# First attention unit taken pair of heads by pair of heads, in a fused attention and two-MoE kernel

## The chip, the cores and the metric

The kernel runs on one core of a Trainium2 chip. The metric is device time in microseconds, the median of three runs. Five engines work side by side, each through its own list of instructions in order: TensorE (PE; its weight loads are PEld), VectorE (DVE), ScalarE (ACT), GpSimd (POOL) and SyncE (SP, which issues most transfers). They wait for each other by semaphores.

## The reference

```python
kv = np.einsum('bhsd,bhse->bhde', k, v)           # linear attention, 4 batches, 8 heads, 576 rows, width 64
out = np.einsum('bhsd,bhde->bhse', q, kv)
x = out / sqrt(mean(out * out) + 1e-6) * g_norm    # then 2304 rows of 512 (8 heads x 64)
# first MoE, dense: 4 experts, hidden 1024, p = domain_probs / sum
out += p[:, e:e + 1] * (np.maximum(x @ w1[e], 0.0) @ w2[e])
# second MoE: 8 experts, one chosen per row by cosine logits; its softmax weight times relu(x @ w1) @ w2
```

## The kernel before, in words

All matmuls of the two MoEs work on split numbers: a value is cast to a high part (ACT, line 61), and the rest is the low part (VectorE or POOL, line 62). Each product is then three matmuls: high by high, high by low, low by high.

The 2304 rows are six units of 384 rows, three tiles of 128 each. The first layer of a unit and half an expert is four blocks (hidden slices of 128) of 12 matmuls each, 128x384 (line 802, `plain_unit`); relu and split of the hidden values are lines 786 and 789. The second layer takes each tile in two halves of six matmuls, 128x512 (line 909, `l2_unit`); line 915 scales its result by the normalized probabilities into the accumulator the first time, line 918 adds to it later. From the second pair of units on, a Strassen scheme (line 814) replaces the plain blocks.

The program's order is written by hand: `run_steps` takes a list of TensorE steps, each with a nominal length, and puts the entries of `todo` behind the step at which their due time has passed. So the due times set the order in each engine's list, not the moment at which something runs. `att(tiles)` makes the attention of a tile a series of such entries: `qt_unit` (transpose q, line 142; copy by ACT, line 148; it also asks for a later q tile), `x_unit` (state product, line 159; square, line 173; sum, line 175; root, line 186), `x_norm` (lines 187 to 198 and 181) and `xt_unit` (transpose, line 204; ACT's scaled copy, line 208). `x_norm` is spread over the list behind its `x_unit`, and the next tile's `qt_unit` stands ahead of the previous tile's `xt_unit`.

Weights come by a stream of transfers through four buffers (`issue`, lines 551 to 567; w1 at line 560, w2 at line 564). A buffer is asked for again when its block has been split, so SP waits for VectorE, and what is behind it in SP's list waits too. `take` hands out the blocks in stream order.

The first unit has code of its own (lines 983 to 1038). The stream's first four blocks are k and v of batch 0, one pair of heads each: four rows of a head side by side in a partition, and the last 64 rows of all heads apart (`load_tail`, line 96). `kv_unit` multiplies k and v of a pair over the rows (lines 107 and 110) and copies the result into a block-diagonal state (line 113). Then the three tiles of q are transposed, multiplied by the state (line 159), squared, summed and normalized together, transposed and split into the first-layer input (lines 204, 211, 212). `heat` are matmuls whose result nobody reads. k and v of batch 1 go into `en_b`, a buffer that later holds the second MoE's embeddings; their four `kv_unit`s stand between the four blocks of the first unit's first layer (due at 1.5, 3.5, 5.5, 7.5), and the split of the second-layer weights (`fill_w2`) and the normalization of the probabilities `dp` (`norm_probs`, lines 1041 to 1044) stand there too. Tile 3's attention runs beside the second layer of the first phase; tiles 4 and 5 beside the next phase, which is the same unit with the other half of the expert.

Of the kernel before, what the change touches and what calls it, by code (L numbers as in the profile page):

```python
# [20 lines left out]
def attn_moe_moe_kernel(ctx: ExitStack, tc: tile.TileContext, q, k, v, g_norm, dprobs, w1, w2, emb, tau, w1b, w2b, out):  # L21
# [646 lines left out]
    stream += [("kv", 0, n) for n in range(NP)] + raws(0, 0) + raws(0, 1) + raws(0, 0)  # L668
# [280 lines left out]
    def run_steps(steps, todo, pace):  # L949
        todo = sorted(todo, key=lambda x: x[0])  # L950
        at = 0.0
# [32 lines left out]
    for _ in range(RAW):  # L984
        issue()
    Q0 = TS

    def q_first_raw(t):
        return xr.rearrange("p u c n -> p (u c n)")[:, D * t:D * t + D]

    for t in range(Q0):
        load_q(t, nc.sync, q_first_raw(t))
    for m in kv_bd:
        nc.gpsimd.memset(m, 0.0)
    for i in range(2):
        nc.gpsimd.dma_start(out=g2[64 * i:64 * i + 64], in_=g_norm.rearrange("(d o) -> d o", o=1))
    for p in range(NP):
        kv_unit(0, p)
        heat(2)
    def load_kv1(p):  # L1000
        load_kv(1, p, en_b[:, 2 * p:2 * p + 2].rearrange("p i n -> p (i n)"))

    load_tail(1)
    for p in range(NP):
        load_kv1(p)
    nc.sync.dma_start(out=dp, in_=dprobs.rearrange("(t p) e -> p t e", p=128))
    for t in range(Q0, Q0 + QB):
        load_q(t, nc.sync)
    qx = [acc[TS + t].rearrange("p (a n) -> p a n", a=NP) for t in range(Q0)]
    px = [psp.tile([128, H, DH], F32, name=f"psx{t}", tag=("x0", "x1", "l20")[t]) for t in range(Q0)]  # L1010
    ms = st_p.tile([128, TS, H], F32, name="ms3", tag="ms3", bufs=1)

    def q_first(t):
        ps = q_transpose(t, ("tp", "l10", "l11")[t])
        (nc.vector.tensor_copy if t % 2 == 0 else nc.scalar.copy)(qx[t], ps)

    def x_first(t):
        x_mm(t, qx[t], px[t])
        x_s[t] = acc[t].rearrange("p (h d) -> p h d", h=H)
        nc.scalar.activation(out=x_s[t], in_=px[t], func=ACTF.Square)  # L1020
        nc.vector.tensor_reduce(out=ms[:, t], in_=x_s[t], axis=AX.X, op=ALU.add)

    q_first(0)
    q_first(1)
    for t in range(Q0):
        if t + 2 < Q0:
            q_first(t + 2)
        x_first(t)
    heat(14, psp.tile([128, 128], F32, name="warm2", tag="kv"))
    ri = rms_end(*rms_start(ms, [128, TS, H], "s"))  # L1030
    w1_blocks(0, 0)
    for part in range(3):
# [278 lines left out]
```

## Time and profile before

| | |
|---|---|
| median of three runs | 1152.33 us (1151.47 to 1153.69) |
| the profiled execution | 1154.61 us, span 1152.7 us |
| busy in the span | PE 1110.8 us (96%), DVE 764.9 (66%), ACT 559.5 (49%), POOL 276.4 (24%) |
| mean granted TensorE clock | 0.989 of full speed |

The span is the time from the first to the last instruction; the profiled execution's time is 1.9 us longer. A timeline row gives start and length in us, the engine, the line, what is written from what, and how often; in brackets stands how long the engine was idle before and what ended that wait. A matmul's length holds its way through the array, so rates are read from start to start. A float32 matmul shows as two records, a transpose as one. Between 0 and 80 us TensorE is idle for the loads, for the first unit's normalization, and twice for 1.4 us for an attention tile; after that it hardly waits until the routing at 840 us.

### The profile page before, as it was taken

To read this page: it belongs to the slowest core of one execution; us is meant where nothing else is said; L and a number is where in the kernel's file an instruction comes from. 1 tells how busy PE (TensorE), PEld (TensorE's weight loads), DVE (VectorE), ACT (ScalarE), POOL (GpSimd) and SP (SyncE) were. 2 spreads that over 40 slices of the span, in tenths; PEclk is the share of its full clock that TensorE was granted. 3 is DMA by queue.
4 is the path that set the end of the run, shared out by engine and by line. 5 is a ranking of instruction groups with operands and counts; after the bars stand their busy time and mean duration, and the time that the engine had idled before them with its cause. 6 is when DMAs were issued, how large, how long until landed. Compare 5 with 4: busy or idle time off the path is not lost. (4 is left out here: it accounts for less than half of the span.)

```text
span 1152.7 us, 17304 instructions
## 1 busy us (share of the span) xinstructions
PE 1110.8 (96%) x5905; PEld 972.7 (84%) x5905; DVE 764.9 (66%) x1340; ACT 559.5 (49%) x1000; POOL 276.4 (24%) x325
## 2 busy tenths in 40 slices
PE   7999999999999999999999999999968999999996
PEld 7889898888888898889889998899857878888875
DVE  3467665566996788766796787765876548763662
ACT  3545446444455344444455444332336348763663
POOL 3002332222441322322243322200011112112111
PEclk9999999999999999999999999999989999999999
DMA  9523244221334232221232222123164159855871
GB/s 263 142 55 110 83 147 149 72 82 47 107 113 142 88 92 63 67 74 56 82 119 83 82 83 65 55 73 119 37 240 135 38 163 376 315 172 169 281 239 43
DMA packets 89730, 141.79 MB, mean 123 GB/s; under 512 B 17365, under 2 KB 52181, under 8 KB 89504
## 3 DMA queue, kind: packets, MB, share of 16 engines
q1 hardware_dynamic: 82032, 115.66, 31.1%
q0 software_dynamic: 7600, 24.93, 6.5%
q8 instruction: 49, 0.80, 0.3%
q14 instruction: 49, 0.40, 0.1%
HBM read 178.31 MB, written 10.49 MB: 164 GB/s over the span
## 5 line engine op out<-in xcount | busy, mean ns | idle before, releaser
L909 PE MATMUL bank<-w2h,hh 128*128 128x512 f32 x576 | 227.4, 395 | 1.4 <-ACT hh L786 1.4
L909 PE MATMUL bank<-w2h,hl 128*128 128x512 f32 x576 | 225.5, 391 | 0.0
L909 PE MATMUL bank<-w2l,hh 128*128 128x512 f32 x576 | 225.0, 391 | 0.0
L62 DVE TENSOR_TENSOR w2l<-raw,w2h 128x1024 fp32r<-128x1024 f32 x100 | 120.3, 1225 | 91.5 <-ACT w2h L61 90.9
L814 PE MATMUL bank<-xth,w1h 128*128 128x384 f32 x560 | 145.9, 341 | 5.5 <-ACT s L821 2.6
L814 PE MATMUL bank<-xth,w1l 128*128 128x384 f32 x560 | 142.6, 335 | 0.0
L814 PE MATMUL bank<-xtl,w1h 128*128 128x384 f32 x560 | 142.5, 335 | 0.0
L918 DVE SCALAR_TENSOR_TENSOR acc<-bank,dp,acc 128x512 f32<-128x512 f32 x123 | 91.9, 747 | 59.9 <-PE bank L909 59.6
L909 PEld LDWEIGHTS bank<-w2h,hl 128*128 128x128 f32 x576 | 108.1, 188 | 24.8 <-DVE hl L789 1.8
L909 PEld LDWEIGHTS bank<-w2h,hh 128*128 128x128 f32 x576 | 108.2, 188 | 24.5 <-ACT hh L786 3.7
L909 PEld LDWEIGHTS bank<-w2l,hh 128*128 128x128 f32 x576 | 108.2, 188 | 21.0
L814 PEld LDWEIGHTS bank<-xth,w1h 128*128 128x128 f32 x560 | 99.3, 188 | 11.0 <-ACT s L821 3.8
L62 DVE TENSOR_TENSOR w1l<-raw,w1h 128x512 fp32r<-128x512 f32 (+2 forms) x137 | 89.5, 669 | 22.5 <-ACT w1h L61 22.5
L61 ACT CAST w2h<-raw 128x1024 fp32r<-128x1024 f32 x100 | 102.9, 1056 | 1.8 <-DMA raw<-in_moe_w_dram 0.8
L814 PEld LDWEIGHTS bank<-xtl,w1h 128*128 128x128 f32 x560 | 101.4, 188 | 0.0
L814 PEld LDWEIGHTS bank<-xth,w1l 128*128 128x128 f32 x560 | 101.2, 188 | 0.0
L825 POOL TENSOR_TENSOR sv<-sv,s 128x384 f32<-128x384 f32 x40 | 45.8, 1145 | 202.0 <-ACT sv L821 193.2
L314 DVE CUSTOM_DVE_ANT_0 scr<-row,en_b 128x512 bf16<-128x512 f32 x112 | 86.5, 772 | 9.3 <-DMA row<-x1d 8.8
L821 ACT COPY s<-bank 128x384 f32<-128x384 f32 x80 | 38.3, 479 | 83.2 <-PE bank L814 83.1
L1207 POOL DMA_INDIRECT out_dram<-y,ix x22 | 22.6, 1025 | 223.1 <-ACT y L1206 104.0
L61 ACT CAST w1h<-raw 128x512 fp32r<-128x512 f32 (+2 forms) x140 | 73.9, 572 | 0.0
L61 ACT CAST w1h<-wsum 128x1024 fp32r<-128x1024 f32 x40 | 41.9, 1048 | 63.2 <-POOL wsum L609 63.2
(255 smaller groups left out, 1990.6 us busy)
## 6 DMA issues: line engine op xcount, KB each, us to landing
raw<-in_moe_w_dram SPq DMA_DIRECT2D x290, 512.0 KB
x1d<-acc POOLq DMA_DIRECT2D x15, 256.0 KB, 2.3
row<-x1d POOLq DMA_DIRECT2D x14, 256.0 KB, 3.1
raw<-in_k_dram SPq DMA_DIRECT2D x12, 256.0 KB
raw<-in_v_dram SPq DMA_DIRECT2D x12, 256.0 KB
qraw<-in_q_dram POOLq DMA_DIRECT2D x12, 256.0 KB, 3.9
en_b<-in_moe_expert_emb_dram POOLq DMA_DIRECT2D x1, 2048.0 KB
en_b<-in_k_dram SPq DMA_DIRECT2D x4, 256.0 KB
```

The costliest lines, as they stand in the source:

```text
L61: nc.scalar.copy(hi, raw)
L62: (eng or nc.vector).tensor_tensor(out=lo, in0=raw, in1=hi.bitcast(F32), op=ALU.subtract)
L314: nc.vector.tensor_tensor_reduce(out=scr, in0=x, in1=en_b[:, e], scale=1.0, scalar=0.0, op0=ALU.mult, op1=ALU.add, accum_out=lg[:, t, e:e + 1]
L814: nc.tensor.matmul(out=ps, lhsT=wform(wo, b, w)[:, c], rhs=xform(xo, x)[:, c], start=start and n == 0, stop=(n == 5), skip_group_check=True)
L821: nc.scalar.copy(t, src)
L825: (eng or nc.vector).tensor_tensor(out=out, in0=a, in1=b, op=ALU.add)
L909: nc.tensor.matmul(out=ps, lhsT=h_t[o][f][u][:, ns], rhs=w[j][:, a], start=(k == 0 and m == 0), stop=(k == 3 and m == 2))
L918: nc.vector.scalar_tensor_tensor(out=fin, in0=ps, scalar=dp[:, t, e:e + 1], in1=ac, op0=ALU.mult, op1=ALU.add)
L1207: nc.gpsimd.indirect_dma_start(out=out[:, :], out_offset=bass.IndirectOffsetOnAxis(ap=ix[:, col(s):col(s) + 1], axis=0), in_=y, in_offset= ...
```

## The change

The first unit's k, v and q are loaded by pairs of heads, six rows of a head side by side in 96 partitions, so the tail disappears; k and v of batch 0 leave the weight stream and lie in `en_b` and in six buffers of the later Strassen sums. The eight query loads, one per head, are issued by ACT. Each pair goes through product, state product, square and sum alone (`pair_product`), with six `heat` matmuls behind it; normalization and transposes follow one and two pairs later. The first layer of this unit is taken pair by pair as well: six matmuls per pair and two blocks (`first_layer`), into four accumulators that stay open. First-layer weights are split by VectorE, where POOL did one block of them.

k and v of batch 1 and the probabilities are loaded after the first layer's code, behind the third and fourth weight blocks of the stream and in front of the next second-layer weights. The four products of batch 1 move to the next phase (due at 4.0 to 5.5), and tiles 4 and 5 there are spread over 6 to 14 instead of 0 to 13.

```diff
-    stream += [("kv", 0, n) for n in range(NP)] + raws(0, 0) + raws(0, 1) + raws(0, 0)
+    stream += raws(0, 0) + raws(0, 1) + raws(0, 0)
...
-    def run_steps(steps, todo, pace):
+    def run_steps(steps, todo, pace, at=0.0):
         todo = sorted(todo, key=lambda x: x[0])
-        at = 0.0
         for n, (d, fn) in zip(pace, steps):
             fn()
             at += d
...
-    for _ in range(RAW):
+    Q0 = TS
+    ROWS = 6
+    en_flat = en_b.rearrange("p e n -> p (e n)")
...
+    q_pair = [xr.rearrange("p u c n -> p (u c n)")[:, SUB * p:SUB * p + SUB].rearrange("p (t h d) -> p t h d", t=TS, h=2) for p in range(NP)]
+
+    def load_first(p):
+        for s, src in enumerate((k, v)):
+            a = 4 * p + 2 * s
+            if a + 2 <= 10:
+                nc.sync.dma_start(
+                    out=en_flat[0:S // ROWS, SUB * a:SUB * a + 2 * SUB].rearrange("p (h x) -> p h x", h=2),
+                    in_=src[0, 2 * p:2 * p + 2].rearrange("h (p r) d -> p h (r d)", r=ROWS),
+                )
+            else:
+                for i in range(2):
+                    nc.sync.dma_start(out=h_raw[a + i].rearrange("p (r d) -> p r d", r=ROWS), in_=src[0, 2 * p + i].rearrange("(p r) d -> p r d", r=ROWS))
+
+    for p in range(NP):
+        for i in range(2):
+            nc.scalar.dma_start(out=q_pair[p][:, :, i], in_=q[0, 2 * p + i, 0:SUB, :].rearrange("(t p) d -> p t d", t=TS))
+    for p in range(NP - 1):
+        load_first(p)
+    issue()
+    load_first(NP - 1)
+    for _ in range(RAW - 1):
         issue()
...
+    for t in range(Q0, Q0 + QB):
+        load_q(t, nc.sync)
...
+    def load_kv1():
+        load_tail(1)
+        for p in range(NP):
+            load_kv(1, p, en_b[:, 2 * p:2 * p + 2].rearrange("p i n -> p (i n)"))
...
+    def pair_product(p):
+        r = h_raw[4 * p:4 * p + 4]
+        ps = psp.tile([128, DH], F32, name="pskv", tag="kv")
+        for c in range(ROWS):
+            for i in range(2):
+                nc.tensor.matmul(out=ps[64 * i:64 * i + 64], lhsT=r[i][:, DH * c:DH * c + DH], rhs=r[2 + i][:, DH * c:DH * c + DH], start=(c == 0), stop=(c == ROWS - 1))
+        for i in range(2):
+            sl = slice(64 * i, 64 * i + 64)
+            nc.scalar.copy(kv_bd[0][sl, p, sl], ps[sl])
+        pq = psp.tile([128, TS, 128], F32, name="psq", tag="tp")
+        for t in range(TS):
+            nc.tensor.transpose(pq[:, t], q_pair[p][:, t].rearrange("p h d -> p (h d)"), ident)
+        qs = acc[2 + p][:, 0:SUB].rearrange("p (t n) -> p t n", t=TS)
+        nc.scalar.copy(qs, pq)
+        px = psp.tile([128, TS, 2, DH], F32, name="psx", tag=f"x{p % 2}")
+        for t in range(TS):
+            nc.tensor.matmul(out=px[:, t].rearrange("p h d -> p (h d)"), lhsT=qs[:, t], rhs=kv_bd[0][:, p], start=True, stop=True)
+        xs = (acc[p][:, 0:SUB] if p < 2 else spare[:, SUB * p - 2 * SUB:SUB * p - SUB]).rearrange("p (a d) -> p a d", d=DH)
+        px = px.rearrange("p t h d -> p (t h) d")
+        nc.scalar.activation(out=xs, in_=px, func=ACTF.Square)
+        ms = st_p.tile([128, 2 * TS], F32, name="msp", tag=f"msp{p}", bufs=1)
+        nc.vector.tensor_reduce(out=ms, in_=xs, axis=AX.X, op=ALU.add)
+        first[p] = (px, xs, rms_start(ms, [128, 2 * TS], f"p{p}"))
+
+    def pair_norm(p):
+        px, xs, st = first[p]
+        ri = rms_end(*st)
+        nc.vector.tensor_tensor(out=xs, in0=px, in1=ri.unsqueeze(2).to_broadcast([128, 2 * TS, DH]), op=ALU.mult)
+
+    def pair_xt(p):
+        xs = first[p][1]
+        ps = psp.tile([128, TS, 128], F32, name="psxt", tag=("l20", "kv", "tp", "kv")[p])
+        for t in range(TS):
+            nc.tensor.transpose(ps[:, t], xs[:, 2 * t:2 * t + 2].rearrange("p h d -> p (h d)"), ident)
+        hi, lo = (a[:, SUB * p:SUB * p + SUB] for a in xf_t)
+        ps = ps.rearrange("p t n -> p (t n)")
+        nc.scalar.activation(out=hi, in_=ps, func=ACTF.Copy, scale=g2[:, 0:1])
+        nc.vector.scalar_tensor_tensor(out=lo, in0=ps, scalar=g2[:, 0:1], in1=hi.bitcast(F32), op0=ALU.mult, op1=ALU.subtract)
...
+    def first_layer(p, n):
+
+        j, c = divmod(p, 2)
+        for i in range(2):
+            f = 2 * n + i
+            if len(first_ps) == f:
+                first_ps.append(bank()[:, 0:SUB])
+            for m, (wo, xo) in enumerate(((0, 0), (1, 0), (0, 1))):
+                nc.tensor.matmul(
+                    out=first_ps[f], lhsT=wform(wo, n, ((0, 1), (3, 2))[i][j])[:, c], rhs=xform(xo, j)[:, c],
+                    start=(p == 0 and m == 0), stop=(p == NP - 1 and m == 2),
+                )
+            if p == NP - 1:
+                h_hi(f, 0, first_ps[f])
+                h_lo(f, 0, first_ps[f])
+
+    def first_weights(n):
+        w1_blocks(0, n)
+        for part in range(3):
+            w1_direct(n, part, more=part < 2)
...
     for p in range(NP):
-        kv_unit(0, p)
-        heat(2)
-    def load_kv1(p):
-        load_kv(1, p, en_b[:, 2 * p:2 * p + 2].rearrange("p i n -> p (i n)"))
-
-    load_tail(1)
-    for p in range(NP):
-        load_kv1(p)
-    nc.sync.dma_start(out=dp, in_=dprobs.rearrange("(t p) e -> p t e", p=128))
-    for t in range(Q0, Q0 + QB):
-        load_q(t, nc.sync)
...
-    q_first(0)
-    q_first(1)
-    for t in range(Q0):
-        if t + 2 < Q0:
-            q_first(t + 2)
-        x_first(t)
-    heat(14, psp.tile([128, 128], F32, name="warm2", tag="kv"))
-    ri = rms_end(*rms_start(ms, [128, TS, H], "s"))
-    w1_blocks(0, 0)
-    for part in range(3):
-        w1_direct(0, part, nc.gpsimd)
-    for t in range(TS):
-        nc.vector.tensor_tensor(out=x_s[t], in0=px[t], in1=ri[:, t].unsqueeze(2).to_broadcast([128, H, DH]), op=ALU.mult)
-    for t in range(TS):
-        xt_unit(t, ("tp", "l10", "l11")[t], first=True)
-    issue()
+        pair_product(p)
+        heat(6)
+        if p:
+            pair_norm(p - 1)
+        if p > 1:
+            pair_xt(p - 2)
+        if p == 2:
+            first_weights(0)
+    pair_xt(2)
+    first_layer(0, 0)
+    pair_norm(3)
+    first_layer(1, 0)
+    first_weights(1)
+    first_layer(2, 0)
+    pair_xt(3)
+    for p in range(NP - 1):
+        first_layer(p, 1)
+    for n in range(2):
+        first_layer(NP - 1, n)
+
...
-    def plain_phase(un, e, fh, todo, pace):
-        steps = [(P1T / 4, lambda f=f: plain_unit(un % 2, f)) for f in range(4)]
+    def plain_phase(un, e, fh, todo, pace, begun=False):
+        steps = [] if begun else [(P1T / 4, lambda f=f: plain_unit(un % 2, f)) for f in range(4)]
         steps += l2_steps(e, fh, [un], None, first_half, (P2T - P1T) / 6)
-        run_steps(steps, todo, pace)
+        run_steps(steps, todo, pace, P1T if begun else 0.0)
...
-    w1_blocks(0, 1)
-    todo = w2_fills(0, 0) + [(-1, f) for f in plain_direct(1)]
-    todo += [(1.5 + 2 * p, lambda p=p: kv_unit(1, p)) for p in range(NP)] + [(6.0, norm_probs)]
-    todo += [(10.0 + c, lambda c=c: nc.vector.tensor_tensor(
+    load_kv1()
+    nc.sync.dma_start(out=dp, in_=dprobs.rearrange("(t p) e -> p t e", p=128))
+    for n in range(2):
+        fill_w2(0, n)
+    norm_probs()
+    todo = [(10.0 + c, lambda c=c: nc.vector.tensor_tensor(
         out=xr[:, 0, c], in0=xform(0, 0, 2)[:, c].bitcast(F32), in1=xform(1, 0, 2)[:, c].bitcast(F32), op=ALU.add)) for c in range(NC)]
-    plain_phase(0, 0, 0, todo + w1_plain_fills(0, 1) + spread(att([TS]), 9, P2T), [0] * 99)
-    todo = w2_fills(0, 1) + spread(att(range(TS + 1, 2 * TS)), 0, 13)
-    plain_phase(0, 0, 1, todo + [(13.2, lambda: x_split(6, xblock(0, 1))), (14.5, xs_f["b22"])], [0] * 99)
+    plain_phase(0, 0, 0, todo + w1_plain_fills(0, 1) + spread(att([TS]), 9, P2T), [0] * 99, True)
+    todo = w2_fills(0, 1) + [(4.0 + 0.5 * p, lambda p=p: kv_unit(1, p)) for p in range(NP)] + spread(att(range(TS + 1, 2 * TS)), 6, 14)
+    plain_phase(0, 0, 1, todo + [(14.2, lambda: x_split(6, xblock(0, 1))), (15.2, xs_f["b22"])], [0] * 99)
```

On ACT, around the end of the first unit's first layer, `hh` are the high parts of its four hidden blocks, `w2h` those of the second-layer weights, `acc` the first scaled results. Before:

```order
L786 ACTIVATE hh_125<-bank 128x384
L61 CAST w1h<-raw 128x512
L61 CAST w1h<-raw 128x256 x2
L113 COPY kvbd_143<-pskv 64x64 x2
L61 CAST w2h_85<-raw 128x1024
L786 ACTIVATE hh_127<-bank 128x384
L113 COPY kvbd_143<-pskv 64x64 x2
```

After:

```order
L786 ACTIVATE hh_129<-bank 128x384
L786 ACTIVATE hh_131<-bank 128x384
L61 CAST w2h_85<-raw 128x1024
L61 CAST w2h_86<-raw 128x1024
L61 CAST w1h<-raw 128x512
L915 ACTIVATE acc_119<-bank,dp 128x512
L148 COPY qT<-psq 128x512
```

The first cast of second-layer weights stood behind the first of the four hidden blocks and now stands behind the last.

On TensorE, where the first unit passes from attention to its first layer, `acc` and `wsum` hold normalized states, `psxt` their transposes. Before:

```order
L142 MATMUL psq<-ident,xr 128x128 x12
L159 MATMUL psx_295<-kvbd_142,acc_122 128x128 x4
L159 MATMUL psx_296<-kvbd_142,acc_123 128x128 x4
L159 MATMUL psx_297<-kvbd_142,acc_124 128x128 x4
L981 MATMUL warm_335<-ident 128x128 x14
L204 MATMUL psxt<-ident,acc_119 128x128 x4
L204 MATMUL psxt<-ident,acc_120 128x128 x4
L204 MATMUL psxt<-ident,acc_121 128x128 x4
L802 MATMUL bank<-xth,w1h 128x384 x4
```

After:

```order
L1032 MATMUL pskv<-sv,su 64x64 x12
L1038 MATMUL psq<-ident,xr 128x128 x3
L1043 MATMUL psx<-kvbd_142,acc_124 128x128 x3
L980 MATMUL warm<-ident 128x128 x6
L1060 MATMUL psxt<-ident,acc_120 128x128 x3
L1060 MATMUL psxt<-ident,wsum 128x128 x3
L1074 MATMUL bank<-xth,w1h 128x384
```

The last pair's product, state product and warming matmuls are followed by the transposes of the second and third pair, and only then by the first layer.

On TensorE, in the middle of the next phase (second half of expert 0), `pskv` are the products of batch 1, `psq` and `psx` tile 4's query transposes and state product. Before:

```order
L802 MATMUL bank<-xth,w1h 128x384 x4
L802 MATMUL bank<-xth,w1l 128x384 x4
L802 MATMUL bank<-xtl,w1h 128x384 x4
L142 MATMUL psq<-ident,qraw 128x128 x4
L802 MATMUL bank<-xth,w1h 128x384 x4
L802 MATMUL bank<-xth,w1l 128x384 x4
L802 MATMUL bank<-xtl,w1h 128x384 x4
L159 MATMUL psx<-kvbd_142,qT 64x128 x4
L159 MATMUL psx<-kvbd_143,qT 64x128 x4
```

After:

```order
L107 MATMUL pskv<-en_b 64x64 x8
L110 MATMUL pskv<-kvtail 64x64 x2
L107 MATMUL pskv<-en_b 64x64 x8
L110 MATMUL pskv<-kvtail 64x64 x2
L107 MATMUL pskv<-en_b 64x64 x8
L110 MATMUL pskv<-kvtail 64x64 x2
L802 MATMUL bank<-xth,w1h 128x384 x4
L802 MATMUL bank<-xth,w1l 128x384 x4
L802 MATMUL bank<-xtl,w1h 128x384 x4
L142 MATMUL psq<-ident,qraw 128x128 x4
L159 MATMUL psx<-kvbd_142,qT 64x128 x4
L159 MATMUL psx<-kvbd_143,qT 64x128 x4
```

Three products now stand in a row, and the state product of tile 4 follows its query transposes with no block between them; tile 5's state product and its transposes have six second-layer matmuls between them, where there were twelve.

## Rows read from the trace of the kernel before

**Rows 1.** The page's costliest groups: one eviction 384 wide (busy, mean ns; idle before).

```profile
L821 ACT COPY s<-bank 128x384 f32<-128x384 f32 x80 | 38.3, 479 | 83.2 <-PE bank L814 83.1
```

**Rows 2.** Windows: busy us per engine (count), PEclk, DMA share, GB/s.

```profile
10.00:12.00 2.00, 2.00 (x42) 1.68 (x39) 0.00 (x0) 0.41 (x2) 0.00 (x0) 1.00 1.16 341
...
22.00:24.00 2.00, 0.33 (x4) 0.14 (x3) 1.85 (x4) 0.00 (x0) 2.00 (x3) 1.00 1.17 174
...
26.00:31.00 5.00, 4.09 (x12) 3.70 (x12) 1.42 (x3) 0.55 (x1) 1.68 (x7) 0.50 0.91 228
```

**Rows 3.** Timeline, first unit: start, us, engine, line, operation, count [idle before, releaser].

```profile
7.89 0.69 PE L107 MATMUL pskv<-raw 128*64 128x64 f32 x16 [1.35 <-DMA raw<-in_v_dram]
...
8.95 0.42 ACT L113 COPY kvbd<-pskv 64x64 f32<-64x64 f32 x2 [6.70 <-PE pskv L110]
...
15.80 0.66 PE L142 MATMUL psq<-ident,xr 128*128 128x128 f32 x4 [0.33 <-DMA xr<-in_q_dram]
...
16.29 2.84 PE L159 MATMUL psx<-kvbd,acc 128*128 128x128 f32 x24
...
18.97 3.29 PE L981 MATMUL warm<-ident 128*128 128x128 f32 x28
...
23.93 1.89 PE L204 MATMUL psxt<-ident,acc 128*128 128x128 f32 x12 [1.67 <-DVE acc L1035]
```

**Rows 4.** Timeline, SP's second-batch and probability loads, and their use.

```profile
14.96 1.36 SPq L96 DMA_DIRECT2D kvtail<-in_k_dram  x1
...
25.55 0.47 SPq L1006 DMA_DIRECT2D dp<-in_moe_domain_probs_dram  x1
...
31.01 0.94 PEld L107 LDWEIGHTS pskv<-en_b 128*64 128x64 f32 x16 [0.44 <-DMA dp<-in_moe_domain_probs_dram]
...
39.03 0.22 DVE L1041 TENSOR_REDUCE sm<-dp 128x18 f32<-128x72 f32 x1
...
39.79 0.23 DVE L1044 TENSOR_TENSOR dp<-dp,sm 128x72 f32<-128x72 f32 x1
```

**Rows 5.** Timeline, first layer of the first unit into its second layer.

```profile
33.10 1.05 ACT L61 CAST w2h<-raw 128x1024 fp32r<-128x1024 f32 x1
...
34.19 1.23 DVE L62 TENSOR_TENSOR w2l<-raw,w2h 128x1024 fp32r<-128x1024 f32 x1 [0.67 <-ACT w2h L61]
...
35.64 0.96 PE L802 MATMUL bank<-xth,w1h 128*128 128x384 f32 x4
...
37.92 0.55 PEld L107 LDWEIGHTS pskv<-en_b 128*64 128x64 f32 x16 [0.25 <-issue]
...
38.80 0.96 PE L802 MATMUL bank<-xth,w1h 128*128 128x384 f32 x4
...
41.96 0.50 PE L909 MATMUL bank<-w2h,hh 128*128 128x512 f32 x1
...
44.84 0.60 PE L142 MATMUL psq<-ident,qraw 128*128 128x128 f32 x4
...
45.03 0.69 ACT L915 ACTIVATE acc<-bank,dp 128x512 f32<-128x512 f32 x1 [1.89 <-PE bank L909]
...
45.62 0.58 ACT L148 COPY qT<-psq 128x512 f32<-128x512 f32 x1
...
46.67 1.05 PE L159 MATMUL psx<-kvbd,qT 128*128 128x128 f32 x8
```

**Rows 6.** Timeline, attention tiles beside the first two second layers.

```profile
53.29 0.66 PE L204 MATMUL psxt<-ident,xs 128*128 128x128 f32 x4 [1.45 <-DVE xs L181]
...
58.51 1.58 PE L159 MATMUL psx<-kvbd,qT 128*64 128x128 f32 x16
...
62.84 0.69 DVE L181 TENSOR_TENSOR xs<-psx,rs 128x512 f32<-128x512 f32 x1
...
66.57 1.05 PE L159 MATMUL psx<-kvbd,qT 128*128 128x128 f32 x8
...
71.79 0.63 PE L204 MATMUL psxt<-ident,xs 128*128 128x128 f32 x4 [1.41 <-DVE xs L181]
```

More of the change, by code (lines that the diff above doesn't have):

```diff
@@ L983, in attn_moe_moe_kernel @@
     heat(14)
-    for _ in range(RAW):
-        issue()
-    Q0 = TS
-    def q_first_raw(t):
-        return xr.rearrange("p u c n -> p (u c n)")[:, D * t:D * t + D]
-    for t in range(Q0):
-        load_q(t, nc.sync, q_first_raw(t))
+    Q0 = TS
+    ROWS = 6
+    en_flat = en_b.rearrange("p e n -> p (e n)")
+    h_raw = [en_flat[0:S // ROWS, SUB * i:SUB * i + SUB] for i in range(10)]
+    h_raw += [sum_p.tile([128, SUB], F32, name=n, tag=n, bufs=2)[0:S // ROWS] for n in ("s1", "su", "sv") for _ in range(2)]
+    q_pair = [xr.rearrange("p u c n -> p (u c n)")[:, SUB * p:SUB * p + SUB].rearrange("p (t h d) -> p t h d", t=TS, h=2) for p in range(NP)]
[18 more added lines that the diff above has]
+    for _ in range(RAW - 1):
+        issue()
+    for t in range(Q0, Q0 + QB):
+        load_q(t, nc.sync)
     for m in kv_bd:
@@ L996, in attn_moe_moe_kernel @@
         nc.gpsimd.dma_start(out=g2[64 * i:64 * i + 64], in_=g_norm.rearrange("(d o) -> d o", o=1))
-    for p in range(NP):
-        kv_unit(0, p)
-        heat(2)
-    def load_kv1(p):
-        load_kv(1, p, en_b[:, 2 * p:2 * p + 2].rearrange("p i n -> p (i n)"))
-    load_tail(1)
-    for p in range(NP):
-        load_kv1(p)
-    nc.sync.dma_start(out=dp, in_=dprobs.rearrange("(t p) e -> p t e", p=128))
-    for t in range(Q0, Q0 + QB):
-        load_q(t, nc.sync)
-    qx = [acc[TS + t].rearrange("p (a n) -> p a n", a=NP) for t in range(Q0)]
@@ L1010, in attn_moe_moe_kernel @@
[L1010 to L1021, printed above, removed]
@@ L1023, in attn_moe_moe_kernel @@
-    q_first(0)
-    q_first(1)
-    for t in range(Q0):
-        if t + 2 < Q0:
-            q_first(t + 2)
-        x_first(t)
-    heat(14, psp.tile([128, 128], F32, name="warm2", tag="kv"))
-    ri = rms_end(*rms_start(ms, [128, TS, H], "s"))
-    w1_blocks(0, 0)
-    for part in range(3):
-        w1_direct(0, part, nc.gpsimd)
-    for t in range(TS):
-        nc.vector.tensor_tensor(out=x_s[t], in0=px[t], in1=ri[:, t].unsqueeze(2).to_broadcast([128, H, DH]), op=ALU.mult)
-    for t in range(TS):
-        xt_unit(t, ("tp", "l10", "l11")[t], first=True)
@@ L1038, in attn_moe_moe_kernel @@
-    issue()
+    def load_kv1():
+        load_tail(1)
+        for p in range(NP):
+            load_kv(1, p, en_b[:, 2 * p:2 * p + 2].rearrange("p i n -> p (i n)"))
+    first, first_ps = {}, []
+    spare = sum_p.tile([128, 4, 2, 128], F32, name="wsum", tag="wsum").rearrange("p a b c -> p (a b c)")
+    def pair_product(p):
[21 more added lines that the diff above has]
+        first[p] = (px, xs, rms_start(ms, [128, 2 * TS], f"p{p}"))
@@ new lines, in first_weights @@
+    def first_weights(n):
+        w1_blocks(0, n)
+        for part in range(3):
+            w1_direct(n, part, more=part < 2)
+    turn4[0] = 0
+    for p in range(NP):
+        pair_product(p)
[15 more added lines that the diff above has]
+        first_layer(p, 1)
```

## The prediction

> **What bounds the kernel now.** I read the page first: TensorE is busy 96% of the span, and the chain that ended last runs through it, so an edit is worth what it does to TensorE's waiting, and an early shift carries to the end one for one unless a later wait swallows it. I take none to do so, because transfers and splits run ahead of TensorE from the second unit on. Then I read the timeline of the first 80 us engine by engine. Four stretches show there.
>
> The first is 0 to 27 us. The four pair products follow the loads, and the last query tile lands as late as 15.80; then the normalization chain holds TensorE 1.67 us ahead of the transposes [rows 3]. [...]
>
> The second is the first layer. Its second block takes 12 matmuls from 35.64 to 37.92 less 0.25 idle, 2.03 us or 0.17 us each, and between two blocks one second-batch pair product takes 0.88 us plus that 0.25, 1.13 us [rows 5]. Three such products and the first one, slower at half clock (about 1.4), are 4.8 us of such work before 41.96, so without it the first layer would have ended at 41.96 - 0.2 - 4.8 = 36.95. While it runs, ACT casts and VectorE splits the second-layer weights (33.10 and 34.19, 1.05 and 1.23 us): hidden.
>
> The third is the second layer from 41.96; its attention tile 3 reaches its state product at 46.67, 4.71 us later [rows 5]. The transposes of that tile come at 53.29, 6.62 us after it, with 1.45 us idle [rows 6]. The fourth is the next phase, with tiles 4 and 5 beside it and 1.41 us idle ahead of the last transposes [rows 6].
>
> **The change part by part.** Times are from the span's start, in the profiled run (1154.61 us, 2.3 above the median of the three timed runs; I add the difference to the median). Between engines I take 0.1 us per hop, as between the end of a pair product and its copy in rows 3.
>
> *Pairs.* One pair is now a chain on TensorE: 12 products, ACT's two copies, the query copy, three state matmuls, six warming matmuls. Ten products took 0.95 us, so 12 take 1.0; the copies 0.42 [rows 3]; a 384-wide eviction 0.48 [rows 1]; state matmuls 2.84/12 = 0.24 each and warming ones 3.29/14 = 0.235 each [rows 3]. From its first product: copies done at 1.55, query copy at 2.1, state at 2.9, warming at 4.35. The warming matmuls cover the square and the sum but stand on the path to the next pair, since the loads don't bind: 3.15 MB of k, v, q and 0.52 MB of weights need 2.36/0.341 + 0.79/0.174 + 0.52/0.341 = 13 us at the rates of rows 2 (1 KB runs in the first row, mostly 256-byte ones in the second), so all land by about 17. First pair: 7.89 in before [rows 3] for 0.79 MB; here 0.79 MB too, but ACT issues eight query loads ahead of its first copy. I take 7.5, bounds 6.5 (where the idle 1.35 us ahead of 7.89 begin) and 9. Pairs start at 7.5, 11.85, 16.2, and, with three transposes of 0.5 us (four took 0.66 [rows 6]), 21.05.
>
> *Last pair to the first layer.* ACT's casts of the first weight block stand ahead of the last pair's copies: pair 2 is squared, its root and the first transposed hi part follow, and with casts of 1.2 us ACT is free at 16.2 + 6.7. So the last state product ends at 24.8, not 24.0. After it, square 0.5, sum 0.55, root 0.3, five short VectorE operations of together 1.06 and a product of 0.55 (sizes by 384/512 from the tile chain: from the product's end at 60.09 to 63.53, 3.44 us, for 512) [rows 6] let the transposes of pair 2 start at 28.2, and they stand in front of all first-layer matmuls. From there 24 matmuls, 3 transposes, 24 matmuls: 28.7 + 8.2 + 0.5 = 37.4. Against 36.95 in before: +0.45. The pipelining gains nothing here, because each pair waits for its own evictions where before four pairs were done in one sweep of three tiles. Bounds: 32.1 if TensorE never waits (7.5 + 14.4 for four pairs without hops + 2 + 8.2), 40 if the clock falls.
>
> *Second-layer weights.* They are now split after the first layer's last relu on ACT and VectorE. With the last two relus (as wide as the eviction of rows 1) ACT reaches the cast 0.7 us after the last matmul, then come 1.05, then 1.23 on VectorE [rows 5] until the second matmul may go: 3.15 us after the first layer's end, 2.7 later than the 0.2 plus one matmul of before. This cover is gone for good. +2.7, bounds 0 and 3.
>
> *Second batch and probabilities.* The third weight block waits for the split of the first one, the fourth for that of the second, which VectorE does after the norm of pair 3: 32.7 by the chain above. SP is in order, so the fourth block, the tails, 2.1 MB of k and v, and behind them the probabilities wait for it. At the rates above 0.52, 0.26 and 2.1 MB take 1.5 + 1.5 + 6.2 = 9.2 us, and I add 2 for issue and landing: 44. (In before from the tail's issue at 14.96 to the landing at 31.01, 16 us, with 2 MB of weights ahead [rows 4].) Bounds 40 and 48. Their normalization takes 0.99 us (39.03 to 40.02) [rows 4], and the first accumulation and tile 3's query copy, 0.59 and 0.58 to the start and end of the copy [rows 5], stand behind it on ACT. So tile 3's state product may start at 46.4. TensorE alone reaches it at 37.4 + 0.2 + 2.7 + 4.7 = 45.0. +1.4, bounds 0 and 4. In all it starts at 46.4 where before has 46.67; the chain of 6.62 us behind it is the same.
>
> *Second phase.* The four second-batch products move in. One stands alone (1.13), three in a row: each waits for the copy of the one before, 0.88 + 0.1 + 0.42 + 0.1 = 1.5. 0.25 + 1.5 + 1.5 + 0.88 = 4.1, in all 5.2 against 4.8: +0.4, and since the 4.8 lay ahead of 46.67 in before, this stretch alone grows by 5.2. Tile 4's state product follows its query transposes directly: ACT's relu and query copy (0.48, 0.58) stand between and cost 0.8 us, where before 12 matmuls lay between. From the end of a state product to its norm's end took 3.44 us [rows 6]; tile 4 now has 3.3 us of matmuls in it (0.25 lost), tile 5 six matmuls, 1.37 us, instead of twelve (2.2 lost, against 1.41 now). 0.8 + 0.25 + 2.2 - 1.41 = +1.85, bounds 0 and 4.
>
> *Rest.* The eight smaller query loads on ACT and the early set-up of the routing on POOL lie under the loads of the first 10 us: 0, bounds -0.5 and +1.2.
>
> Sum: 0.45 + 2.7 + 1.4 + 0.4 + 1.85 = **6.8 us**, and 1152.3 + 6.8 = 1159.1.
>
> [...] In before all k, v and q loads stand in one queue, and the first product starts at 7.89 [rows 3]. [...]
>
> **The rivals.** (a) *The clock falls in the new first layer.* It fell after 1.67 us of idle time in before [rows 2, 3]; here TensorE idles about 1.5 us twice, at 22.6 and 26.7. For: nearly the same gap. Against: gaps of 1.45 and 1.41 us in rows 6 were followed by no fall in the page's clock line. Price: five us at half the clock, as in rows 2, without their idle fifth, 2.5, less the 1.4 for the probabilities that then lie beneath: 1.1, so 1160.2; with a second fall behind the new waits up to 1163.
>
> (b) *Not slower: the pairs overlap.* If ACT's copies finish early enough that TensorE never waits between pairs, the first layer ends at 32.1, 5.3 earlier. All loads move with it, and the probabilities bind at 41.2: 5.5 us before 46.67, against 7.05 of growth behind it (5.2 + 1.85): +1.6, 1153.9. It decides from tile 3's state product at about 42 on. Against: every state product needs two copies and an eviction that only start when the products end.
>
> (c) *Faster.* If in (b) the weight splits are hidden and the probabilities early as well, the state product stands at 37.0, 9.7 earlier: -2.6, 1149.7. Against: ACT's program order has the casts behind the relus.
>
> **How the numbers follow.** The forecast has 0.5 (own range 1156.5 to 1161.5), (a) 0.22, (b) 0.17, (c) 0.11. A measurement can tell 0.2%, 2.3 us, from no change: below 1150.0 is (c), 1150.0 to 1154.6 is (b) without its upper tail, to which I add the lower tail of the forecast. Faster 0.11, same 0.17, slower 0.72. The range for 8 in 10 reaches from 1152, which leaves out (c), to 1162.5, which leaves out the two-fold fall of the clock.
>
> **What would show it.** The pair products' starts 4.3 us apart; transposes of pair 2 at about 28 with idle time released by VectorE ahead of them; the second layer's second matmul released by the split of the low part, some 3 us after the last first-layer matmul; ACT's first scaled accumulation released by the normalization of the probabilities at about 45; three second-batch products in a row 1.5 us apart; over 2 us idle ahead of tile 5's transposes; and the start of the second unit's first layer near 83 us. I am wrong if the second layer starts before 33 us, or if the second phase is not about 7 us longer than now.

## The result, and the profile after

The changed kernel took 1161.75 us (1159.66 to 1166.31) against 1152.06 us: 1.0085 of the time before, 95% interval 1.0068 to 1.0102, or +9.7 us. The forecast was +6.8 us. The profiled execution took 1163.84 us, its span is 1162.1 us. These rows of its timeline answer to [rows 3]: start, length, engine, line, what is written from what, count, and in brackets the idle time before and what ended it.

```profile
0.93 1.51 ACTq L1004 DMA_DIRECT2D xr<-in_q_dram  x3
...
2.46 5.87 ACTq L1004 DMA_DIRECT2D xr<-in_q_dram  x5
...
6.96 0.92 PE L1032 MATMUL pskv<-en_b 96*64 96x64 f32 x24
...
8.44 0.42 ACT L1035 COPY kvbd<-pskv 64x64 f32<-64x64 f32 x2 [6.18 <-PE psq L1038]
...
9.51 0.91 PE L1043 MATMUL psx<-kvbd,acc 128*128 128x128 f32 x6 [1.16 <-ACT acc L1040]
...
11.69 0.92 PE L1032 MATMUL pskv<-en_b 96*64 96x64 f32 x24
...
15.86 0.92 PE L1032 MATMUL pskv<-s,en_b 96*64 96x64 f32 x24
...
20.37 0.92 PE L1032 MATMUL pskv<-sv,su 96*64 96x64 f32 x24
...
23.05 0.94 PE L1043 MATMUL psx<-kvbd,acc 128*128 128x128 f32 x6 [1.29 <-ACT acc L1040]
...
27.09 0.52 PE L1060 MATMUL psxt<-ident,wsum 128*128 128x128 f32 x3 [1.44 <-DVE wsum L1054]
```

The pairs' products start 4.73, 4.17 and 4.51 us apart, and in each pair TensorE waits for ACT before the state matmuls. The transposes of pair 2 wait for VectorE and start at 27.09, where about 28 was forecast. Rows marked ACTq or SPq are loads being issued: the eight query loads fill ACT's list from 0.93 to 8.33.

The next rows, from the first layer's last matmul to attention tile 3, answer to [rows 4] and [rows 5].

```profile
35.99 0.34 PE L1074 MATMUL bank<-xtl,w1h 128*128 128x384 f32 x1
...
36.76 1.98 ACT L61 CAST w2h<-raw 128x1024 fp32r<-128x1024 f32 x2
...
37.64 0.44 SPq L1159 DMA_DIRECT2D dp<-in_moe_domain_probs_dram  x1
...
37.84 0.51 PE L909 MATMUL bank<-w2h,hh 128*128 128x512 f32 x1 [1.51 <-ACT w2h L61]
...
39.10 0.51 PE L909 MATMUL bank<-w2l,hh 128*128 128x512 f32 x1 [0.76 <-DVE w2l L62]
...
43.53 0.23 DVE L1111 TENSOR_REDUCE sm<-dp 128x18 f32<-128x72 f32 x1 [3.35 <-DMA dp<-in_moe_domain_probs_dram]
...
44.63 0.69 ACT L915 ACTIVATE acc<-bank,dp 128x512 f32<-128x512 f32 x1 [5.38 <-DVE dp L1114]
...
45.22 0.58 ACT L148 COPY qT<-psq 128x512 f32<-128x512 f32 x1
...
45.85 1.16 PE L159 MATMUL psx<-kvbd,qT 128*128 128x128 f32 x8 [0.51 <-ACT qT L148]
```

Both new waits are there. The second matmul of the second layer starts 3.11 us after the first layer's last one, held by the cast and then by the split. The probabilities are issued at 37.64 and read at 43.53, and ACT's first scaled result, and behind it tile 3's query copy, wait for them. The rows of the second phase answer to [rows 6].

```profile
52.99 0.96 PE L802 MATMUL bank<-xth,w1h 128*128 128x384 f32 x4
...
57.35 0.69 PE L107 MATMUL pskv<-en_b 128*64 128x64 f32 x16
...
60.51 0.69 PE L107 MATMUL pskv<-en_b 128*64 128x64 f32 x16
...
61.98 0.69 PE L107 MATMUL pskv<-en_b 128*64 128x64 f32 x16 [0.53 <-ACT kvbd L113]
...
63.46 0.69 PE L107 MATMUL pskv<-en_b 128*64 128x64 f32 x16 [0.53 <-ACT kvbd L113]
...
67.88 1.58 PE L159 MATMUL psx<-kvbd,qT 128*64 128x128 f32 x16 [0.73 <-ACT qT L148]
...
79.52 0.63 PE L204 MATMUL psxt<-ident,xs 128*128 128x128 f32 x4 [2.19 <-DVE xs L181]
...
82.74 0.87 PE L802 MATMUL bank<-xth,w1h 128*128 128x384 f32 x4
```

The same places in the profile of before, from the first layer of the first unit on:

```profile
26.91 1.62 PE L802 MATMUL bank<-xth,w1h 128*128 128x384 f32 x4 [1.08 <-DVE xtl L212]
...
53.70 0.95 PE L802 MATMUL bank<-xth,w1h 128*128 128x384 f32 x4
...
76.40 0.87 PE L802 MATMUL bank<-xth,w1h 128*128 128x384 f32 x4
```

The phase lasts from 52.99 to 82.74, 29.75 us; before it was 53.70 to 76.40, 22.70. That is the forecast growth of 7.05, with the products 1.47 apart and 2.19 us idle ahead of tile 5's transposes. The second unit starts at 82.74 where "near 83" was forecast, a shift of 6.34. So this trace bears the steps of the second phase and both new waits out, and yet the median grew by over 3 us more than this shift.

### The profile page after: what moved, and what is told of

Same layout as the page of the kernel before. It is cut to its first block, busy times and chain, and to the rows that moved or that the text cites. A ratio compares the mean times of both kernels' runs of the same rounds, so it can differ in the third digit from the quotient of the medians.

```text
span 1162.1 us, 17393 instructions
## 1 busy us (share of the span) xinstructions
PE 1114.2 (96%) x5925; PEld 974.5 (84%) x5925; DVE 767.4 (66%) x1359; ACT 562.3 (48%) x1008; POOL 274.6 (24%) x322
## 5 line engine op out<-in xcount | busy, mean ns | idle before, releaser
L814 PEld LDWEIGHTS bank<-xth,w1h 128*128 128x128 f32 x560 | 99.3, 188 | 10.2 <-ACT s L821 3.8
```

The source lines that it names most:

```text
L814: nc.tensor.matmul(out=ps, lhsT=wform(wo, b, w)[:, c], rhs=xform(xo, x)[:, c], start=start and n == 0, stop=(n == 5), skip_group_check=True)
```

## The experiments

Below, "mark" is the start of the second unit's first layer. Three profiles of the changed kernel were taken in all (two of them under the labels below), and three of the one before.

**The changed kernel again, and its two early waits.** First the kernel once more, beside the next three on one chip.

> The changed kernel unaltered, beside the same runs of before. Theory: 6.3 us of its loss stand at the start of the second unit's first layer (82.74 us against 76.40 in the first profiles), the rest comes after 850 us from the stretch in which the granted clock is down behind the routing's two idle gaps, and differs from run to run. So 1159 to 1166, start of the second unit near 82.7. Rival: the rest is a fixed cost of the change; then the profile shows it at the same place and size, 2.5 us between 860 and 873 us.

1161.55 us, 1.0076 (1.0060 to 1.0093), mark at 82.80. In this profile the clock stayed at 1.00 from 40 to 44 us, where it was 0.50 in the first one; tile 3's state product started at 45.91 all the same, after 2.21 us of waiting in place of 0.51:

```profile
45.91 1.16 PE L159 MATMUL psx<-kvbd,qT 128*128 128x128 f32 x8 [2.21 <-ACT qT L148]
```

The probabilities set that start, and the slower clock lay beneath them.

Next, the second-layer weights are split in the middle of the first layer, with the order of the transfers kept:

```diff
     pair_xt(3)
+    for n in range(2):
+        split(w2h[n].rearrange("p a d -> p (a d)"), w2l[n].rearrange("p a d -> p (a d)"), take("w2", 0, n))
     for p in range(NP - 1):
...
     for n in range(2):
-        fill_w2(0, n)
+        issue()
```

> The changed kernel with the split of the first second-layer weights placed before the last pair's first-layer matmuls on ACT and VectorE; the transfers keep their order. Theory: the probabilities bind behind it (tile 3's state product started at 45.85, released by the query copy behind them), so TensorE's waits of 1.51 and 0.76 us for these splits vanish, but the wait ahead of that state product grows from 0.51 to some 3 to 4.5, and the start of the second unit moves by less than 0.7 us. Rival: the splits cost their 2.3 to 2.9 us; second unit's start near 80, time 2.5 lower.

1165.12 us, 1.0114 (1.0096 to 1.0133). VectorE's and TensorE's rows at tile 3:

```profile
43.77 0.23 DVE L1113 TENSOR_REDUCE sm<-dp 128x18 f32<-128x72 f32 x1 [6.62 <-DMA dp<-in_moe_domain_probs_dram]
...
46.09 2.07 PE L159 MATMUL psx<-kvbd,qT 128*128 128x128 f32 x8 [5.45 <-ACT qT L148]
```

TensorE stands ready at 40.64, where the repeat had 43.70 (0.28 of that is an earlier first layer). The time saved turns into waiting, 5.45 in place of 2.21 us, and the state product starts no earlier. So far the expectation holds. But behind the wait the clock fell to 0.50 from 45.8 us on, and the mark came at 84.28, 1.5 later than in the repeat, where less than 0.7 was expected. The profile is the fastest of its five executions (1161.84). The other four took over 3 us more, and their mean granted clock was lower, 0.985 against 0.989; where in them it was down wasn't profiled.

Then the other half: the load of the probabilities in front of the third weight block.

```diff
+    nc.sync.dma_start(out=dp, in_=dprobs.rearrange("(t p) e -> p t e", p=128))
     for m in kv_bd:
...
     load_kv1()
-    nc.sync.dma_start(out=dp, in_=dprobs.rearrange("(t p) e -> p t e", p=128))
```

> The changed kernel with the load of the probabilities in front of the third weight block instead of behind batch 1's k and v. Theory: alone it is worth only the 0.51 us that TensorE waited ahead of tile 3's state product, since the late splits bind next: state product at 45.3, second unit's start 82.2. Rival: the probabilities cost their whole wait on ACT, 5.38 us, and the time falls by 4 or 5.

1160.74 us, 1.0068 (1.0048 to 1.0088). Tile 3's state product no longer waits:

```profile
43.23 1.05 PE L159 MATMUL psx<-kvbd,qT 128*128 128x128 f32 x8
```

It starts 2.68 earlier than in the repeat, and the second phase at 50.26, against 53.05. The 0.5 us expected was the wait of the first profile, in which a stretch at half clock lay beneath it. The clock fell from 77.7 to 81.1, behind the 2.19 us wait for tile 5, and took 1.57 us back (that phase was 31.32 us long), so the mark is at 81.58. And both edits together:

> The changed kernel with both: early split and early probabilities. Theory: the two together are worth far more than the sum, for either covers the other: state product of tile 3 near 41.1 (first layer's end 36.2, plus 0.2, plus 4.7), second unit's start near 78, time about 4.5 lower than the changed kernel, 1157. Rival: the two gains add up, under 1 us by the theory's single values or 7 by the rival's.

1156.17 us, 1.0033 (1.0020 to 1.0045): 5.4 us less than the repeat. TensorE's rows:

```profile
36.03 0.39 PE L909 MATMUL bank<-w2h,hh 128*128 128x512 f32 x1
...
36.26 0.40 PE L909 MATMUL bank<-w2l,hh 128*128 128x512 f32 x1
...
40.62 1.05 PE L159 MATMUL psx<-kvbd,qT 128*128 128x128 f32 x8
...
47.24 0.66 PE L204 MATMUL psxt<-ident,xs 128*128 128x128 f32 x4 [1.46 <-DVE xs L181]
```

The second layer follows without a gap and tile 3 starts 5.29 earlier than in the repeat: 2.68 for the probabilities and 2.61 for the splits. The first layers of the three profiles start up to 0.4 us apart (27.36, 26.98, 27.23); counted from there, the two are 2.30 and 2.86. The two waits were in a row, and the later one hid the other; removed alone, the splits gave nothing.

**The second phase.** The four second-batch products go to the second layer of the first phase, two of them into the wait ahead of tile 3's transposes, and tiles 4 and 5 are spread from the phase's start again, as in the kernel before.

```diff
-    plain_phase(0, 0, 0, todo + w1_plain_fills(0, 1) + spread(att([TS]), 9, P2T), [0] * 99, True)
-    todo = w2_fills(0, 1) + [(4.0 + 0.5 * p, lambda p=p: kv_unit(1, p)) for p in range(NP)] + spread(att(range(TS + 1, 2 * TS)), 6, 14)
-    plain_phase(0, 0, 1, todo + [(14.2, lambda: x_split(6, xblock(0, 1))), (15.2, xs_f["b22"])], [0] * 99)
+    plain_phase(0, 0, 0, todo + w1_plain_fills(0, 1) + spread(att([TS]), 9, P2T) + [((13.0, 14.5, 15.3, 15.5)[p], lambda p=p: kv_unit(1, p)) for p in range(NP)], [0] * 99, True)
+    todo = w2_fills(0, 1) + spread(att(range(TS + 1, 2 * TS)), 0, 13)
+    plain_phase(0, 0, 1, todo + [(13.2, lambda: x_split(6, xblock(0, 1))), (14.5, xs_f["b22"])], [0] * 99)
```

> The kernel after, with the second batch's four state products (PE L107, L110) taken from the second unit-phase's first layer into the second layer of the first unit's first phase, the last two of them between the second layer and the transposes that wait 1.44 us for the VectorE, and with tiles 4 and 5 spread from the phase's start again (0 to 13 in place of 6 to 14). Theory (the second phase's growth of 7.05 us is the four products plus the squeeze of tiles 4 and 5 behind them): the second phase falls from 29.75 to about 22.7 us, the first phase grows by four products of about 0.85 us less the 1.44 us that two of them cover, about +2.0; the second unit's first layer starts near 77.7 (82.74 in the kernel after), time about 1156.5. Rival (the tiles 4 and 5 are late because their loads or ScalarE's 0.5 us copies are late, not because of their place): the second phase stays above 27 us, the products cost 3.4 us in the first phase, time 1160 or more.

1156.74 us, 1.0033 (1.0021 to 1.0046), the expected time, with the mark 2 us later than expected.

```profile
56.97 0.95 PE L802 MATMUL bank<-xth,w1h 128*128 128x384 f32 x4
...
79.65 0.87 PE L802 MATMUL bank<-xth,w1h 128*128 128x384 f32 x4
```

The second phase is 22.68 us long: the whole 7.05 us was the place of the products and the squeeze behind them. The first phase grew by more than the expected 2.0, by 3.9, with the clock at 0.50 from 46.6 us on.

> The same together with both earlier edits (second-layer weights split in the first layer, domain probabilities loaded in front of the third weight block). Theory (three separate terms make the whole slowdown): first phase ends at 47.66 plus 2.0 = 49.7, second phase 22.7, the second unit's first layer at about 72.4 against 76.40 in the kernel before, so faster than before: 1148 to 1150. Rival (what is left of the slowdown lies in the pair-by-pair start itself): second unit's first layer no earlier than 76, time 1152 or more.

1150.83 us, 0.9987 (0.9975 to 0.9999): faster than before, by little and by an interval that only just leaves out no change. The second phase starts at 50.83, the second unit at 73.54, both 1.1 later than expected: the moved products cost 3.2 us in the first phase, not 2.0. No stretch of its first 48 us has the clock under 1.00.

```profile
40.76 1.05 PE L159 MATMUL psx<-kvbd,qT 128*128 128x128 f32 x8
...
50.42 0.66 PE L204 MATMUL psxt<-ident,xs 128*128 128x128 f32 x4
...
68.93 0.63 PE L204 MATMUL psxt<-ident,xs 128*128 128x128 f32 x4 [1.41 <-DVE xs L181]
```

Tile 3's transposes no longer wait, since products stand there, and tile 5's wait is back at its 1.41 us of before [rows 6]. But 73.54 is 2.86 earlier than the 76.40 of before, and the median only 1.25 better: here, too, the time comes out later than the mark says.

**The pairs' pace.** As the last one, with `heat(2)` for `heat(6)` behind each pair.

> As the one before, and behind each pair's product heat(2) in place of heat(6): 8 warming transposes fewer in each of four pairs, 12 of them took 1.50 us in the kernel after, so 1.0 us a pair. Theory (TensorE's own order sets the pairs' pace, 4.2 to 4.7 us): pairs 3.3 to 3.8 apart, first layer 3 to 4 us earlier, time about 1145.5. Rival 1 (the pairs' loads or ScalarE's copies set the pace): pairs still over 4 us apart, waits on the ScalarE's copy grow by what the heat loses, time as the kernel before it. Rival 2 (the granted clock falls to 0.50 in the pairs or the first layer without the heat): 4 us or more slower than the kernel before it.

1151.03 us, 0.9982 (0.9970 to 0.9994), the same as the one before it, where 1145.5 was expected. Its pairs start 3.41, 3.28 and 4.42 us apart, but the waits behind them take it back:

```profile
16.30 0.91 PE L1044 MATMUL psx<-kvbd,acc 128*128 128x128 f32 x6 [1.24 <-DVE acc L1055]
...
21.12 0.94 PE L1044 MATMUL psx<-kvbd,acc 128*128 128x128 f32 x6 [1.81 <-ACT acc L1041]
...
25.16 0.52 PE L1061 MATMUL psxt<-ident,wsum 128*128 128x128 f32 x3 [2.33 <-DVE wsum L1055]
```

The first layer starts 1.94 earlier (25.43 against 27.37), and in its first matmuls the clock is 0.50 from 26 to 30 us: the 24 ahead of the last pair's transposes take 4.78 us, 1.55 more than in the run before it. The second phase starts 0.40 earlier. Rivals 1 and 2 each take a part.

**Where the other 3 us are.** A first suspicion was the routing, behind 840 us, where the shift grew from 5.6 to 8.2 us. There TensorE waits 5.2 and then 4.1 us, and the clock goes to 0.50. Windows of the first profile of after (length, busy time per engine, granted clock, DMA share, GB/s):

```profile
855.00:860.00 5.00, 1.64 (x11) 1.00 (x10) 4.55 (x17) 0.55 (x1) 2.03 (x2) 0.50 0.29 97
860.00:865.00 5.00, 4.23 (x14) 3.48 (x15) 3.16 (x4) 2.74 (x5) 0.95 (x1) 0.50 0.96 342
865.00:870.00 5.00, 5.00 (x18) 4.28 (x17) 1.12 (x2) 0.21 (x1) 0.00 (x0) 0.53 1.02 400
```

and the same times in the kernel before, whose routing comes 5.6 us earlier:

```profile
855.00:860.00 5.00, 4.91 (x23) 4.22 (x24) 3.24 (x4) 2.73 (x5) 0.94 (x1) 0.65 0.97 360
860.00:865.00 5.00, 4.75 (x23) 3.58 (x22) 2.19 (x4) 3.38 (x6) 0.00 (x0) 1.00 1.03 402
```

Is it the shift alone that makes this stretch longer? The kernel before was shifted with work that nobody reads:

```diff
-    heat(14, psp.tile([128, 128], F32, name="warm2", tag="kv"))
+    heat(59, psp.tile([128, 128], F32, name="warm2", tag="kv"))
```

> The kernel before, with 45 more warming transposes (heat 59 in place of 14) in front of the first unit's transposes: 28 of them took 3.29 us there, so a delay of about 5.3 us for 45 if one heat is one transpose of 0.117 us, or 10.6 us if it is two, less the 1.67 us of waiting that they cover and what the clock gives back; nothing behind the first unit changes. It asks whether the kernel after's loss behind 850 us (+2.7 us on top of its shift of 6.3) comes from the shift alone. If so: time is before plus the shift at the second unit's first layer plus about 2.7, with the stretch at clock 0.50 behind the routing's two waits some 16 us long. If the loss is the kernel after's own: time is before plus that shift, the stretch at 0.50 about 10 us long.

Its mark is at 82.16, 5.76 later than in the profile of before, and its median 1161.67 us, 1.0076 (1.0056 to 1.0097): +9.6, as much as the change, from a kernel in which nothing else differs. But the stretch at 0.50 in its routing was short, 10.2 us, and its span only 6.3 longer than that of the profile of before. So its median lies nearly 4 us further from that of before than its mark does, without anything of the change, and without that longer stretch. What does differ is the first phase: from first layer to second phase it took 24.36 us (35.12 to 59.48), in the profile of before 26.79 (26.91 to 53.70). The clock stood at 1.00 there in every half microsecond from 35 to 48 us, and the 1.67 us wait of [rows 3] was filled by the added work. Fill just that wait in the kernel before, then, and look at it twice more as it is:

```diff
-    heat(14, psp.tile([128, 128], F32, name="warm2", tag="kv"))
+    heat(21, psp.tile([128, 128], F32, name="warm2", tag="kv"))
```

> The kernel before, with 7 more warming steps (heat 21 in place of 14; 28 transposes of 14 steps took 3.29 us, so 1.65 us) that fill the 1.67 us TensorE waited for the VectorE at 23.93; nothing else changes. In the profile of before the clock was 0.50 from 25.7 to 32.4 us behind that wait, which cost about 2.4 us against the profile of b1_shift, where it stayed at 1.00 (first layer to second phase 26.79 against 24.36 us). Theory A (that fall is not in the usual run of the kernel before, so its profile was 2.4 us slower than its median and the forecast stood on too late a base): the fall is gone, the second unit's first layer is near 74 in this profile, and the median is that of before within 0.5 us, 1152. Theory B (the fall is in every run of before): the median is 2 us or more faster, 1149.5 to 1150.

> The kernel before once more, one profile. Theory A: no fall of the clock before 40 us, the second unit's first layer starts near 74.0 in place of 76.40. Theory B: clock 0.50 for 3 us or more between 25 and 33 us, second unit at 75 or later.

> The same kernel, a third profile, with the same two expectations; and the stretch at clock 0.50 behind the two waits of the routing (5.2 and 4.1 us, near 850): 10.3 us if its length is the kernel's own, 13 or 17 us if it varies from run to run.

With the wait filled: 1151.98 us, 1.0001 (0.9990 to 1.0011), no fall, mark at 73.94. The kernel before, unchanged: one execution of 1151.65 us with the mark at 73.93, one of 1154.36 with the mark at 76.87. The window of [rows 2] that showed 0.50, here in the faster of these two:

```profile
26.00:31.00 5.00, 4.11 (x37) 3.75 (x38) 2.61 (x6) 2.22 (x6) 1.67 (x7) 1.00 0.89 218
```

and in the slower one:

```profile
26.00:31.00 5.00, 4.15 (x15) 3.78 (x14) 2.10 (x3) 1.19 (x2) 2.18 (x12) 0.50 0.99 309
```

Both waited the same 1.67 us ahead of it. The faster one is as theory A expects, the slower one as theory B: the fall belongs to some executions and not to others, and it costs 2.3 to 2.4 us (first layer to second phase 26.79 and 26.69 us with it, 24.38 without). For the median, theory A holds: if the usual execution had the fall, filling the wait would have made the median that much faster; it left it as it was. The mean granted clocks fit: it was 0.989 and 0.987 in the two profiles of before with the fall, 0.990 in the one without, and 34 of 60 timed runs of before have 0.990 or more. The profile on which the forecast stood (1154.61 us) had it. TensorE in the execution without:

```profile
23.92 1.85 PE L204 MATMUL psxt<-ident,acc 128*128 128x128 f32 x12 [1.67 <-DVE acc L1035]
...
26.89 0.93 PE L802 MATMUL bank<-xth,w1h 128*128 128x384 f32 x4 [1.12 <-DVE xtl L212]
...
44.23 1.05 PE L159 MATMUL psx<-kvbd,qT 128*128 128x128 f32 x8
...
51.27 0.95 PE L802 MATMUL bank<-xth,w1h 128*128 128x384 f32 x4
...
73.93 0.87 PE L802 MATMUL bank<-xth,w1h 128*128 128x384 f32 x4
```

> The kernel after once more. The stretch at 0.50 in the routing was 17.1 us in both profiles so far, each about 2 us above the kernel's median: 10 or 13.6 us here if it varies from run to run (time then near 1160), 17 again if it is this kernel's own. The second unit's first layer at 82.8 whether or not the clock falls between 40 and 44 us, since the domain probabilities end that wait.

1161.69 us; the mark is at 84.18, with the clock at 0.50 from 79.8 to 83.2 behind tile 5's 2.19 us wait, and so 1.4 later than in the repeat. It was at 0.50 from 38.8 to 42.2 too, which cost nothing: the second phase starts at 52.83. The stretch in the routing was 13.7 us, so its length varies: 17.1, 17.1 and 13.7 us in the three profiles of after, 10.2, 13.7 and 13.7 in those of before.

## Why the prediction was right in sign and short by 3 us

- *Pairs.* Right: 4.35 us forecast, 4.17 to 4.73 measured. The first pair started at 6.96, inside the bounds and earlier than the 7.5 taken, and at 7.36 and 6.26 in the other two profiles: with the query loads issued by ACT it came later than the 7.5 in none of the three. The loads did not bind, as forecast: no pair's products wait for a transfer. But the two rates of [rows 2] were put down to the wrong packets: in the second window 207 of 502 are under 512 bytes, in the first 995 of 1422. What the query loads on ACT did cost is ACT itself: its first copy came at 8.44, 1.48 behind the start of the first product, where in the second pair it is 0.99.
- *Last pair to the first layer.* The transposes of pair 2 came at 27.09, forecast 28.2, and the layer ended near 36.2, not 37.4. The pairs had been earlier all along (the fourth at 20.37, forecast 21.05).
- *Second-layer weights.* +2.7 forecast, 2.61 to 2.86 in the experiment that removes them behind the early probabilities. Rows of after: 3.11 us to the second matmul, 3.15 forecast.
- *Probabilities.* Read at 43.53, forecast 44; the 2 us in that 44 for issue and landing were the author's estimate, which no run shows apart: the rows of after have 5.89 us from the issue at 37.64 to the read, behind batch 1's k and v. Tile 3's product came at 45.85, forecast 46.4. The wait that they add beyond the splits is 2.2 to 2.7 (2.21 in the row of the repeat, 2.30 to 2.68 in the experiment), not 1.4, because TensorE would have been there at 43.7, not at 45.0. So the product's place does not test the terms ahead of it: the first layer ended 1.2 early and this wait was about 1 too small in the forecast, and since the probabilities set the start, the two cancel. That the hit is so close is luck.
- *Second phase.* +7.05 forecast, 7.05 measured, and gone with the placing undone. The waits ahead of tile 4's state product and tile 5's transposes were 0.73 and 2.19, forecast 0.8 and 2.2.
- *The base.* This is the step that failed: "Against 36.95 in before" and "it starts at 46.4 where before has 46.67". Both stand on a first layer whose start ran at half clock, 0.50 from 25.6 to 32.4 us. The working carries the fall openly ("slower at half clock"), then treats it as part of the kernel, and the sentence "I add the difference to the median" adds the result to a median that, by the run with the filled wait, is that of executions without it. Against the execution without the fall, tile 3's product moves from 44.23 to 45.91, +1.7, not -0.3, and the mark from 73.93 to 82.80, +8.9. With the forecast's own 46.4 in it, the sum would have been 46.4 - 44.23 + 7.05 = 9.2.
- *The rest, and what stays open.* 8.9 of the 9.5 to 9.7 us are found so. The shifted kernel lacked the fall as well, 82.16 against 73.93, 8.2 of its 9.6. From the mark to the end of the span twelve of the fourteen profiles take 1075.1 to 1076.8 us, whatever the kernel, and whether the stretch at 0.50 in the routing was 10.2 or 13.7 us long; the two with 17.1 us, both of the changed kernel, take 1078.9 and 1079.4. Ahead of the mark, the fall behind tile 5's wait cost the third profile 1.4. So each of the three profiles of the changed kernel lost 1.4 or 3 us to one of two falls, and a run with neither would take some 1160.3 us (an estimate: 82.80, then 1075.7 as in the third profile, and 1.8 between span and time; its three runs at a mean clock of 0.991 or 0.992 took 1159.66 to 1160.51). That is 8.7 above the 1151.65 of before without a fall. Whether such falls come oftener in a kernel that arrives later stays open: a mean granted clock of 0.991 or more stands in 27 of 60 timed runs of before and in 3 of 13 of the changed kernel.
- *The rivals.* (a) saw the fall of the clock, but in the new first layer and at 1.1 us, where the new waits hide it; its second fall behind a new wait did come, in one of three profiles and for 1.4. It did not ask whether the old kernel's fall comes each time. (b) and (c) fell with the waits of each pair on ACT; with less warming the pairs stand closer, but the waits behind them grow and the time stays the same.

From the execution without the fall the account closes in five pieces: the pair-by-pair start costs +0.7 (tile 3's state product in the kernel with both edits, 40.62, against 44.23 less the four products, an estimate of 3 x 1.13 + 0.88 = 4.3); these four products leave the first phase, -4.3; the splits +2.6, the probabilities +2.7; the second phase +7.1; together 8.8.

## What to carry to other kernels

A profile is one execution. If its time lies 0.2% above the median and a stretch of it ran at half clock, ask what the same stretch takes at full clock before an edit is summed against it; more profiles, or an edit that fills the wait ahead of it, settle it. Work that is moved out of a full stretch costs what its new place makes late: of the 7 us here, nearly 4 were not the moved products, which cost 3.2 in the first phase, but the squeeze of the work behind them and the lack of cover. Two waits in a row must be removed together, or the second one swallows what the first gives.

## What was not expected of the hardware

- The same code with the same idle time of 1.67 us ahead of it ran at clock 1.00 once and at 0.50, for 6.8 us, twice. Waits of 2.18 to 2.21 us ahead of tile 5 were followed by a fall of 3.4 us in three profiles (the early probabilities, both early edits, the third of after) and by none in three others. Near 300 us the first profile of before, the third of before, and the first and third of after have a wait of 1.11 to 1.13 us, with one of 0.52 or 0.53 that ends some 2.4 us before: in the third of after it was followed by some 3.4 us in which second-layer matmuls started 0.43 us apart, against 0.23 later on, and in the other three it was not. The idle time alone does not decide; none of these profiles shows the cause.
- Eight query loads issued by ACT kept its list busy from 0.93 to 8.33 us, 1.51 us for the first three and 5.87 for the other five, and its first copy, at 8.44, stood behind them.
